# A part of the attention exponentials by integer writes on VectorE, shifted copies on GpSimd and a sum on TensorE, in a conformer block

## The chip, the core and the metric

The kernel runs on one core of a Trainium2 chip, in one launch. A core has five engines, each with its own queue of instructions, which it takes in order: TensorE (PE in the profile; its weight loads stand apart as PEld), VectorE (DVE), ScalarE (ACT), GpSimd (POOL) and SyncE (SP, which here only issues DMAs). Matrix products land in PSUM, 128 partitions by 8 banks of 512 fp32 numbers; everything else lives in SBUF. The metric is device time in microseconds, the median of the runs.

## What is computed

Two sequences of 4000 tokens with 144 channels pass a conformer block. Cut to its steps:

```python
B, T, D, K, H = (2, 4000, 144, 5, 4)          # head size 36
h = _layernorm(x);  x = x + 0.5 * (_silu(h @ w_ff1a) @ w_ff1b)      # inner size 576
h = _layernorm(x);  q, k, v = split_heads(h @ w_qkv)
scores = jnp.einsum('bhqd,bhkd->bhqk', q, k) * scale
p = _softmax(scores)
att = jnp.einsum('bhqk,bhkd->bhqd', p, v)
x = x + att @ w_o
h = _layernorm(x) @ w_pw1;  a, b = halves(h)
h = a * _sigmoid(b)
c = depthwise convolution of h with 5 taps, dw
x = x + _silu(c) @ w_pw2
h = _layernorm(x);  x = x + 0.5 * (_silu(h @ w_ff2a) @ w_ff2b)
return _layernorm(x)
```

The scores are 2 x 4 x 4000 x 4000 numbers, and each needs an exponential. No maximum is subtracted ahead of it in the kernel.

## The kernel before

**Tiles.** The 8000 tokens are 16 chunks of 500 (`CH`), eight to a sequence; a chunk is four blocks of 125 tokens (`TB`, `NB`). Attention runs in 32 groups: sequence, query chunk, pair of heads (`groups`). A group walks over 32 key tiles of 125 keys (`NKT`). For one key tile PE makes the scores of 125 keys by 500 queries for two heads with four matmuls (`emit_S`: each head's 64 padded channels take half of the rows of the array, 64 and 61 keys take half of its columns each, so the four lie on different quarters). They go to two PSUM banks; two such pairs, banks 0 to 3, take turns. ACT writes their exponential as bf16 into `PT`, 125 x 1000 in one instruction (`emit_exp`). Four more matmuls multiply by the values `VA` (36 channels and a column of ones, padded to 64) and add up in banks 4 and 5 over the whole group (`emit_O`).

**Epilogue.** At the end of a group, `epilogue` adds banks 4 and 5 on DVE in two instructions (`OTA`, `OTF`), transposes in fp32 on PE, divides by the sum that the column of ones gave, and after the second head pair hands the chunk to `post1` (output projection, norm, gated unit into `U`). `post2` does convolution, second projection, norm, feed-forward, last norm and store. Chunks of the second sequence pass `ff1` and `pre2` (norm, projections to `QT`, `KT`, `VA`) while the first one's attention runs.

**The norm.** `ln` takes statistics on DVE (`ST`, `MV`), raises the variance to the power -1/2 on POOL (two instructions on `RS`), and scales two blocks on DVE into `XN`. There are 160 such half chunks.

**Silu.** While exponentials run, silu and sigmoid are made from tanh (`TH` on ACT, then one DVE instruction), since tanh and exp share a table. Before the attention and after it (`mode["front"]`, `mode["tail"]`) ACT makes silu itself.

**Order.** Nothing is scheduled at run time. A planner, written in Python (`Rec`, `Sched`), writes out the order of each engine before the program is built: every step is a generator that asks for an engine and perhaps a slot; each instruction carries a guessed `cost`, each engine a latency (`LAT`); the step that could start first by these guesses is emitted next. Waits between engines follow from the data. An instruction that comes later than guessed therefore holds up what stands behind it on its engine. During attention only banks 6 and 7 (`banks.restrict`) are left for all side work. All instructions are recorded through one helper, so the profile puts nearly all of them on one line (L135), and they are told apart by the names of their tiles.

**The main loop** alternates between the next score tile and side work. The scores of tile n wait for the exponential of tile n-2. Two series, one of even and one of odd chunks, run `post2`; each takes one chunk to its end before the next. What is left of them when the last key tile is out is emitted after the loop, with all eight banks free. `U` holds all eight chunks of a sequence, `QT` all queries.

Of the kernel before, what the change touches and what calls it, by code (L numbers as in the profile page):

```python
# [6 lines left out]
ALU = mybir.AluOpType  # L7
BF16 = mybir.dt.bfloat16
F32 = mybir.dt.float32

# [10 lines left out]
ATT_SCALE = 0.1669921875  # L21

# [5 lines left out]
class Rec:  # L28
# [5 lines left out]
    LAT = dict(pe=0.2, act=0.2, dve=0.12, pool=0.08, sp=2.0)  # L34
# [10 lines left out]
    def op(self, eng, name, *a, r=(), w=(), q=None, cost=0.1, kind=None, **k):  # L45
# [21 lines left out]
        if eng == "pe":  # L67
            if kind != self.kind:
                start += 0.13
            self.kind = kind  # L70
# [177 lines left out]
def bass_standalone__conformer_family_zipformer__speech_kernel(  # L248
# [29 lines left out]
    NPT = 6  # L278
# [10 lines left out]
    QT = sb("QT", [2, N])  # L289
    KT = sb("KT", [2, N])  # L290
    VA = sb("VA", [NBLK, H, 64])
    PT = sb("PT", [NPT, 2, CH])
    OTA = sb("OTA", [CH], F32)
# [3 lines left out]
    U = sb("U", [CPB, 2, NB, 128])  # L297
# [75 lines left out]
    def va_init(c):  # L373
        blks = slice(c * NB, (c + 1) * NB)
        op("dve", "memset", VA[:, blks, :, DH + 1:64], 0.0, w=[("VA0", c)], cost=0.2)
        op("dve", "memset", VA[:, blks, :, DH:DH + 1], 1.0, w=[("VA1", c)], cost=0.1)
# [54 lines left out]
    def ln(c, g):  # L431
        u = yield need("dve", xnp)
        for i in range(2):
            op("dve", "bn_stats", ST[0:TB, u, i, :], X[0:TB, c * NB + 2 * g + i, :], r=[("X", c, 2 * g + i)],
               w=[("ST", u, i)], cost=0.233)
        yield need("dve")
        for i in range(2):
            op("dve", "bn_aggr", MV[0:TB, u, i, :], ST[0:TB, u, i, :], r=[("ST", u, i)], w=[("MV", u)], cost=0.09)
        op("pool", "tensor_scalar", RS[0:TB, u, :, 1], MV[0:TB, u, :, 1], LN_EPS, None, op0=ALU.add,
           r=[("MV", u)], w=[("VE", u)], cost=0.25)  # L440
        op("pool", "tensor_tensor", RS[0:TB, u, :, 0], RS[0:TB, u, :, 1], NHALF[0:TB, :], op=ALU.pow,
           r=[("VE", u), "NHALF"], w=[("RS", u)], cost=0.6)
        yield need("dve")
        for i in range(2):
            op("dve", "tensor_scalar", XN[0:TB, u, i, :], X[0:TB, c * NB + 2 * g + i, :], MV[0:TB, u, i, 0:1],
               RS[0:TB, u, i, 0:1], op0=ALU.subtract, op1=ALU.mult, r=[("X", c, 2 * g + i), ("MV", u), ("RS", u)],
               w=[("XN", u)], cost=0.25)
        return u
# [64 lines left out]
    def proj(Tt, Wt, nm, c, s, p):  # L513
# [6 lines left out]
        copy(Tt[:, p, c * CH:(c + 1) * CH], PSV[:, bk, 0:CH], [("ps", bk)], [(nm + "T", c)], 0.62, 0.47)  # L520
        banks.give(bk)

    def vproj(c, s, g):
        bk = yield need("pe", banks)
        for i in (2 * g, 2 * g + 1):
            for k in range(2):
# [6 lines left out]
             [("ps", bk), ("VA0", c), ("VA1", c)], [("VA", c)], 0.42, 0.3)  # L533
# [4 lines left out]
    att_done = set()  # L538
# [15 lines left out]
    def pre2(c):  # L554
        s = yield need("dve", xtp, cond=lambda: c in ff1_done)
# [7 lines left out]
        kv_done.add(c)  # L563

    def glu(c, s, hf):
        cc = c % CPB
# [7 lines left out]
        op("dve", "scalar_tensor_tensor", out=U[0:HD, cc, hf, :, 1:1 + TB],  # L574
           in0=TH[0:HD, t, :].rearrange("p (i n) -> p i n", i=NB), scalar=1.0,
           in1=PSV[0:HD, bk, 0:CH].rearrange("p (i n) -> p i n", i=NB), op0=ALU.add, op1=ALU.mult,
           r=[("TH", t), ("ps", bk)], w=[("U", cc)], cost=0.63)
# [3 lines left out]
    def post1(c, a):  # L581
# [13 lines left out]
        yield need("pe", kids=kids, cond=lambda: b == 0 or min(c - CPB + 1, CPB - 1) in conv_done)  # L595
# [4 lines left out]
        xtp.give(s2)  # L600
        if cc == 0:
            op("pool", "memset", U[0:HD, cc, :, 2:4, 0:1], 0.0, w=[("UL", cc)], cost=0.1)
        else:
            op("pool", "tensor_copy", U[0:HD, cc, :, 2:4, 0:1], U[0:HD, cc - 1, :, 2:4, TB:TB + 1],
               r=[("U", cc - 1)], w=[("UL", cc)], cost=0.25)
            op("pool", "tensor_copy", U[0:HD, cc - 1, :, 0:2, TB + 1:TB + 2], U[0:HD, cc, :, 0:2, 1:2],
               r=[("U", cc)], w=[("UR", cc - 1)], cost=0.25)
        if cc == CPB - 1:
            op("pool", "memset", U[0:HD, cc, :, 0:2, TB + 1:TB + 2], 0.0, w=[("UR", cc)], cost=0.1)
        glu_done.add(c)  # L610

    def conv(c, z, hf, silu):
        cc = c % CPB
        bk = yield need("pe", banks)
        o = PSV[0:HD, bk, 0:CH].rearrange("p (i n) -> p i n", i=NB)
        u = U[0:HD, cc, hf, :, :]
        parts = [(2, 0, 4, 0, 1), (1, 1, 4, 0, 1), (1, 0, 1, 3, 0), (0, 2, 4, 0, 1), (0, 0, 2, 2, 0),
                 (3, 0, 3, 1, 1), (3, 3, 4, 0, 2), (4, 0, 2, 2, 1), (4, 2, 4, 0, 2)]
        for j, (tap, i0, i1, s0, off) in enumerate(parts):
            op("pe", "matmul", o[:, i0:i1, :], lhsT=DG[0:HD, hf, tap, :], rhs=u[:, s0:s0 + i1 - i0, off:off + TB],  # L620
               start=j == 0, stop=j == len(parts) - 1, r=[("U", cc), ("UL", cc), ("UR", cc), "DG"], w=[("ps", bk)],
# [49 lines left out]
    def epilogue(b, qc, p, gi):  # L671
        c = b * CPB + qc
        op("dve", "tensor_copy", OTA[:, :], PSV[:, 4, 0:CH], r=[("ps", 4)], w=["OTA"], cost=0.62)
        op("dve", "tensor_tensor", OTF[:, gi % 2, :], PSV[:, 5, 0:CH], OTA[:, :], op=ALU.add, r=[("ps", 5), "OTA"],
           w=[("OTF", gi % 2)], cost=0.62)
# [4 lines left out]
        if p == 0:  # L680
            an_of[c] = yield need("dve", anp)
        a = an_of[c]
        yield need("dve")
# [13 lines left out]
    its = [(gi, kt) for gi in range(len(groups)) for kt in range(NKT)]  # L697
    halves = ((0, 64), (64, TB))
    exps = {}

    def emit_S(n):
        gi, kt = its[n]
        b, qc, p = groups[gi]
        k0 = b * T + kt * TB
        q0 = b * T + qc * CH
        kc, qcc = b * CPB + kt // NB, b * CPB + qc
        for m0, m1 in halves:
            for hh in range(2):
                op("pe", "matmul", PSV[m0:m1, 2 * (n % 2) + hh, 0:CH],
                   lhsT=KT[64 * hh:64 * hh + 64, p, k0 + m0:k0 + m1], rhs=QT[64 * hh:64 * hh + 64, p, q0:q0 + CH],  # L710
                   start=True, stop=True, skip_group_check=True, r=[("WKT", kc), ("WQT", qcc)],
                   w=[("ps", 2 * (n % 2) + hh)], cost=0.0525, kind="q")

    def emit_exp(n):
        s = 2 * (n % 2)
        exps[n] = op("act", "activation", PT[0:TB, n % NPT, :, :], PSV[0:TB, s:s + 2, 0:CH], ACT.Exp, bias=0.0,
                     scale=ATT_SCALE, r=[("ps", s), ("ps", s + 1)], w=[("PT", n % NPT)], cost=0.883)

    def emit_O(n):
        gi, kt = its[n]  # L720
        b, qc, p = groups[gi]
        blk = b * NKT + kt
        for r, (m0, m1) in enumerate(halves):
            for hh in range(2):
                op("pe", "matmul", PSV[64 * hh:64 * hh + 64, 4 + r, 0:CH], lhsT=VA[m0:m1, blk, 2 * p + hh, :],
                   rhs=PT[m0:m1, n % NPT, hh, :], start=kt == 0, stop=kt == NKT - 1, skip_group_check=True,
                   r=[("PT", n % NPT), ("VA", blk // NB)], w=[("ps", 4 + r)], cost=0.0525, kind="q")
        if kt == NKT - 1:
            S.add(epilogue(*groups[gi], gi), first=True)

    def s_start(n):

        gi, kt = its[n]
        b, qc, p = groups[gi]
        kc = b * CPB + kt // NB
        if kc not in kv_done:
            return None
        t = max(R.free["pe"], R.ready(("WKT", kc)), R.ready(("WQT", b * CPB + qc)))
        return max(t, exps[n - 2].done) if n >= 2 else t
# [12 lines left out]
    NIT = len(its)  # L752
    pend = []
    n_s = 0
    n_e = 0
    later = [False]

    def emit_pending(force=False):
        while pend:
            m = pend[0]  # L760
            first = its[m][1] == 0
            t = max(exps[m].done, max(R.ready(("OTF", 0)), R.ready(("OTF", 1))) if first else 0.0)
# [4 lines left out]
    while n_e < NIT:  # L767
        a = s_start(n_s) if n_s < NIT else R.free["pe"]
        t, th = S.best()
        if th is not None and (a is None or t < a or (th.req[0] == "act" and t < a + 0.05)):  # L770
# [8 lines left out]
        assert a is not None, "nothing can go on"  # L779
        if n_s < NIT:  # L780
            emit_S(n_s)
            n_s += 1
        if n_s >= 2 or n_s == NIT:
# [3 lines left out]
            n_e += 1  # L787
    mode["tail"] = True
    emit_pending(force=True)
# [39 lines left out]
```

## Time and profile before

| | |
|---|---|
| median of 3 runs | 1153.02 us |
| the runs | 1148.37 to 1153.84 us |
| span of the profiled execution, first to last instruction | 1145.6 us |
| start of the first exponential | 58.2 us |
| end of the last exponential | 1096.8 us |
| mean granted clock of TensorE | 0.977 |
| HBM read and written | 3.26 MB and 2.30 MB |

The profile gives the profiled execution's span; no other time of that execution is known, and the runs were timed without it. A row of instructions gives engine, operation, written tile and tiles read, shapes, count, then busy time and the mean length of one in ns, then the idle time just before them and who ended it. Instructions of one engine may overlap: the length of one is longer than the distance between the starts of two, for ACT by its pipeline and for PE because a matmul's last rows are still under way when the next one starts. So a price per instruction is read from starts, not from lengths.

### The profile page before, as it was taken

The page shows a single profiled execution, that of the slowest core. Times are in us where ns is not written, and L with a number is a line of the kernel's source. Part 1 is how long each engine was busy: PE and PEld are TensorE (multiplying, and loading weights), DVE is VectorE, ACT ScalarE, POOL GpSimd, SP SyncE. Part 2 cuts the span into 40 slices and gives each one's busy share as a digit, 9 for nine tenths or more (in the row PEclk, how much of TensorE's full clock was granted, in tenths as well). Part 3 has the DMA queues.
Part 4 walks back from the last instruction along what each step waited for, and adds up shares of the span by engine and source line. Part 5 has one row for each costly group of instructions (what it writes and reads, how often), then busy time and mean ns, then how long its engine had stood idle before and what let it go on. Part 6 is the DMA issues. An engine that isn't in the chain of part 4 may idle for free.

```text
span 1145.6 us, 25298 instructions
## 1 busy us (share of the span) xinstructions
PE 959.3 (84%) x10886; PEld 367.5 (32%) x10886; DVE 526.4 (46%) x1657; ACT 1060.9 (93%) x1290; POOL 153.9 (13%) x359
## 2 busy tenths in 40 slices
PE   8998888999999987887879887878878787978766
PEld 3632333333433332322323321322223232323224
DVE  5975655666766643342424520433424241424324
ACT  3789999999999999999999999999999999999942
POOL 3420101111211110010001100100100010101002
PEclk8999999999999999999999999999999999999966
DMA  3000000000000000000000000000000000000000
GB/s 115 2 1 1 1 2 1 1 2 1 7 1 1 7 6 6 2 6 2 1 6 1 9 5 1 1 6 1 6 2 1 6 2 6 2 6 1 6 1 11
DMA packets 8514, 7.18 MB, mean 6 GB/s; under 512 B 1826, under 2 KB 8402, under 8 KB 8402
## 3 DMA queue, kind: packets, MB, share of 16 engines
q1 hardware_dynamic: 7482, 5.11, 1.5%
q8 instruction: 85, 1.39, 0.5%
q10 hardware_dynamic: 920, 0.46, 0.2%
q14 instruction: 27, 0.22, 0.1%
HBM read 3.26 MB, written 2.30 MB: 5 GB/s over the span
## 4 chain that ended last, share of the span: by engine, by line
ACT 68%; PE 23%; DVE 5%; POOL 2%; issue 1%; DMA 1%; ACTq 0%; POOLq 0%; DVEq 0%
ACT PT L135 61%; PE PS L135 23%; ACT TH L135 6%; DVE HT L135 1%; POOL RS L135 1%; DVE XN L135 1%; DVE U L135 1%; DMA WQKV<-in_w_qkv_dram 1%; DVE ST L135 0%; DVE X L135 0%; ACT QT L135 0%; DVE MV L135 0%; DVE VA L135 0%; DVE OTF L135 0%; ACT XT L135 0%
## 5 line engine op out<-in xcount | busy, mean ns | idle before, releaser
L135 ACT ACTIVATE PT<-PS 125x1000 bf16<-125x1000 f32 x1024 | 953.5, 1071 | 12.6 <-PE PS L135 10.3
L135 PE MATMUL PS<-QT,KT 64*64 64x500 bf16 (+1 forms) x4096 | 413.0, 393 | 130.5 <-ACT PT L135 126.5
L135 PE MATMUL PS<-PT,VA 61*64 61x500 bf16 (+1 forms) x4096 | 387.7, 372 | 0.8 <-ACT PT L135 0.8
L135 PEld LDWEIGHTS PS<-QT,KT 64*64 64x64 bf16 (+1 forms) x4096 | 115.4, 103 | 464.4 <-ACT PT L135 424.2
L135 POOL TENSOR_SCALAR RS<-MV 125x2 f32<-125x2 f32 x160 | 34.9, 218 | 883.6 <-DVE MV L135 883.0
L135 PEld LDWEIGHTS PS<-PT,VA 61*64 61x64 bf16 (+1 forms) x4096 | 119.1, 106 | 10.8 <-DVE OTF L135 3.1
L135 DVE COPY OTA<-PS 128x500 f32<-128x500 f32 x32 | 21.7, 679 | 218.0 <-PE PS L135 217.9
L135 POOL TENSOR_TENSOR RS<-RS,NHALF 125x2 f32<-125x2 f32 x160 | 113.9, 712 | 13.4
L135 ACT ACTIVATE TH<-PS 128x500 bf16<-128x500 f32 (+1 forms) x170 | 107.1, 630 | 6.3 <-PE PS L135 6.2
L135 DVE SCALAR_TENSOR_TENSOR HT<-TH,PS 128x500 bf16<-128x500 bf16 x110 | 72.9, 672 | 78.9 <-ACT TH L135 78.8
L135 DVE TENSOR_SCALAR XN<-X,MV,RS 125x144 bf16<-125x144 bf16 x320 | 86.6, 313 | 48.3 <-POOL RS L135 47.5
L135 PE MATMUL PS<-XT,WA 72*128 72x500 bf16 x320 | 93.7, 398 | 9.3 <-DVE HT L135 7.0
L135 DVE SCALAR_TENSOR_TENSOR X<-PS,X 125x288 bf16<-125x288 f32 x128 | 57.2, 448 | 57.0 <-PE PS L135 56.7
L135 DVE BATCH_NORM_STATS2 ST<-X 125x6 f32<-125x144 bf16 x320 | 81.4, 296 | 2.8
L135 DVE COPY XT<-PS 72x500 bf16<-72x500 bf16 x143 | 57.7, 413 | 43.6 <-PE PS L135 43.1
L135 PE MATMUL PS<-WB,HT 128*125 128x144 bf16 x640 | 52.7, 234 | 9.7 <-DVE HT L135 8.8
L135 PE MATMUL PS<-IDENT,XN 125*72 125x125 bf16 x512 | 50.9, 228 | 11.7 <-DVE XN L135 9.3
L135 PEld LDWEIGHTS PS<-WB,HT 128*125 128x125 bf16 x640 | 45.5, 141 | 29.4 <-DVE HT L135 17.3
L135 PEld LDWEIGHTS PS<-IDENT,XN 125*72 125x72 bf16 x512 | 33.7, 115 | 55.9 <-DVE XN L135 32.2
L135 DVE SCALAR_TENSOR_TENSOR U<-TH,PS 72x500 bf16<-72x500 bf16 x32 | 21.5, 671 | 60.0 <-ACT PT L135 30.5
L135 PE MATMUL PS<-U,DG 72*72 72x250 bf16 (+3 forms) x288 | 44.1, 305 | 4.5 <-POOL U L135 3.8
L135 PEld LDWEIGHTS PS<-XT,WA 72*128 72x128 bf16 x320 | 23.4, 101 | 69.0 <-DVE HT L135 29.7
(55 smaller groups left out, 495.0 us busy)
## 6 DMA issues: line engine op xcount, KB each, us to landing
X<-in_x_dram SPq DMA_DIRECT2D x16, 140.6 KB
out_dram<-XN SPq DMA_DIRECT2D x32, 70.3 KB
WA<-in_w_ff1a_dram ACTq DMA_DIRECT2D x1, 162.0 KB
WA<-in_w_ff2a_dram SPq DMA_DIRECT2D x1, 162.0 KB
WB<-in_w_ff1b_dram ACTq DMA_DIRECT2D x1, 144.0 KB
WB<-in_w_ff2b_dram SPq DMA_DIRECT2D x1, 144.0 KB
WQKV<-in_w_qkv_dram ACTq DMA_DIRECT2D x1, 121.5 KB
WP<-in_w_pw_dram SPq DMA_DIRECT2D x1, 81.0 KB
```

The source lines that it names most:

```text
L135: ins = getattr(eng, o.name)(*o.a, **o.k)
```

## The change

134 of the 1024 key tiles leave ACT. They are taken from the last eight key tiles of a group (`NDV`), and are called far tiles here, after the new function `far_tiles`. For such a tile:

- PE makes the scores in banks 6 and 7, which the side work also uses; if only one is free, one head first and the other later.
- DVE computes `LERP_A * score + LERP_B` and writes it as a 16-bit unsigned integer into `PD`, one instruction of 125 x 500 per head. Read as bf16, whose exponent starts at bit 7, such an integer is 2 to a power that is linear in the score, with the fraction replaced by a straight line.
- POOL writes three copies with 32, 64 and 96 added, that is, shifted by a quarter, a half and three quarters of an octave.
- PE multiplies the four with the values and with three scaled copies of the values (`VD`, weights `LERP_W`), sixteen matmuls in all, so that the mean of four shifted lines stands for the exponential. `VD` is made on POOL once for each sequence, for its last eight key tiles.

The planner decides which tile goes this way and when, with two such tiles in flight (`NPD`) and not before the first sequence's keys are all there. Together with this:

- In `ln` the scaling into `XN` moves from DVE to POOL.
- The epilogue's two DVE instructions become one `tensor_reduce` over both banks.
- `VA` keeps 38 columns in place of 64, the output matmuls write 37, and the zero columns aren't set any more; banks 4 and 5 are cleared once by two dummy matmuls.
- `U` holds four chunks (`NUS`) and `QT` twelve (`NQS`), both as rings, and `post1` and `pre2` wait for a free place.
- The order of the four score matmuls is by head, then by half. Some guessed costs and latencies of the planner are new, and the tiles' order in a group may differ.

```diff
-    LAT = dict(pe=0.2, act=0.2, dve=0.12, pool=0.08, sp=2.0)
+    LAT = dict(pe=0.2, act=0.2, dve=0.12, pool=0.15, sp=2.0)
...
+LERP_W = (0.83984375, 0.70703125, 0.59375)
+LERP_A = ATT_SCALE * 128.0 / 0.6931471805599453
+LERP_B = 125.0 * 128.0 - 7.2342
...
-    NPT = 6
+    NPT, NPD, NUS, NQS = 6, 2, 4, 12
+    JT = 4
+    NDV = 8
+    MINREM = 8
+    LEAD = -2
...
-        yield need("dve")
         for i in range(2):
-            op("dve", "tensor_scalar", XN[0:TB, u, i, :], ...
+            op("pool", "tensor_scalar", XN[0:TB, u, i, :], ...
...
     def pre2(c):
...
+        b, k0 = c // CPB, (c % CPB) * NB - (NKT - NDV)
+        if k0 >= 0:
+            for j in range(1, JT):
+                yield need("pool")
+                op("pool", "tensor_scalar", VD[0:TB, b, j - 1, k0:k0 + NB, :, 0:DH + 1],
+                   VA[0:TB, c * NB:(c + 1) * NB, :, 0:DH + 1], LERP_W[j - 1], None, op0=ALU.mult,
+                   r=[("VA", c), ("VA1", c)], w=[("VD", b)], cost=0.8)
+            vd_done.add(c)
...
     def epilogue(b, qc, p, gi):
-        op("dve", "tensor_copy", OTA[:, :], PSV[:, 4, 0:CH], ...
-        op("dve", "tensor_tensor", OTF[:, gi % 2, :], PSV[:, 5, 0:CH], OTA[:, :], op=ALU.add, ...
+        op("dve", "tensor_reduce", out=OTF[:, gi % 2, :], in_=PSV[:, 4:6, 0:CH].rearrange("p b n -> p n b"),
+           axis=mybir.AxisListType.X, op=ALU.add, ...
...
+    def far_tiles(u):
+        while next_tile() is not None or mode["front"]:
+            bk = yield need("pe", banks, cond=lambda: far_tile() is not None)
+            gi, kt = far_tile(take=True)
+            b, qc, p = groups[gi]
+            both = banks.free and banks.best() <= R.free["pe"] + 0.15
+            bks = [bk, banks.take()] if both else [bk]
+            for hh in range(len(bks)):
+                scores(gi, kt, bks[hh], hh)
+            for hh in range(2):
+                if hh == len(bks):
+                    bks.append((yield need("pe", banks)))
+                    scores(gi, kt, bks[hh], hh)
+                yield need("dve")
+                op("dve", "tensor_scalar", PD[0:TB, u, 0, hh, :], PSV[0:TB, bks[hh], 0:CH], LERP_A, LERP_B,
+                   op0=ALU.mult, op1=ALU.add, r=[("ps", bks[hh])], w=[("PD", u)], cost=0.64)
+                banks.give(bks[hh])
+            for j in range(1, JT):
+                yield need("pool")
+                op("pool", "tensor_scalar", PD[0:TB, u, j, :, :], PD[0:TB, u, 0, :, :], float(32 * j), None,
+                   op0=ALU.add, r=[("PD", u)], w=[("PD", u, j)], cost=0.95)
+            vk = kt - (NKT - NDV)
+            pd = PD[:, u, :, :, :].bitcast(BF16)
+            yield need("pe", cond=lambda: o_grp[0] == gi and o_left[gi] < NKT)
+            outputs(gi, [(VA[...] if j == 0 else VD[...], pd[:, j, :, :]) for j in range(JT)], ...)
+            output_done(gi)
```

More of the change, by code (lines that the diff above doesn't have):

```diff
@@ L719, in emit_O @@
     def emit_O(n):
-        gi, kt = its[n]
+        gi, kt = tiles[n]
         b, qc, p = groups[gi]
         blk = b * NKT + kt
[L723 to L727, printed above, removed]
@@ L778, in bass_standalone__conformer_family_zipformer__speech_kernel @@
             continue
[L779 to L783, printed above, removed]
+        assert a is not None and not full, "nothing can go on"
+        more = next_tile() is not None
+        if more:
+            emit_S()
+        if len(tiles) >= 2 or not more:
             emit_exp(n_e)
```

187 lines of the change are left out of this document (127 added, 60 removed).

## The prediction

> **What bounds the kernel now.** I read the page's busy times and groups first, then the windows by stage, then the timeline of a quiet and of a crowded stretch, and the chain of waits at the end.
>
> ```profile
> span 1145.6 us, 25298 instructions
> ...
> PE 959.3 (84%) x10886; PEld 367.5 (32%) x10886; DVE 526.4 (46%) x1657; ACT 1060.9 (93%) x1290; POOL 153.9 (13%) x359
> ...
> L135 ACT ACTIVATE PT<-PS 125x1000 bf16<-125x1000 f32 x1024 | 953.5, 1071 | 12.6 <-PE PS L135 10.3
> ...
> L135 POOL TENSOR_SCALAR RS<-MV 125x2 f32<-125x2 f32 x160 | 34.9, 218 | 883.6 <-DVE MV L135 883.0
> ...
> L135 POOL TENSOR_TENSOR RS<-RS,NHALF 125x2 f32<-125x2 f32 x160 | 113.9, 712 | 13.4
> ...
> L135 DVE TENSOR_SCALAR XN<-X,MV,RS 125x144 bf16<-125x144 bf16 x320 | 86.6, 313 | 48.3 <-POOL RS L135 47.5
> ```
>
> ACT is the full engine, and 1024 exponentials fill it. POOL is nearly empty. The windows (columns: PE, PEld, DVE, ACT, POOL busy, then the granted clock) cut the span at the start of the first exponential, at the end of the first group of 32 key tiles, and at the end of the last exponential; two single groups follow.
>
> ```profile
> 58.20:102.00 43.80, 38.81 (x398) 14.99 (x398) 30.59 (x111) 37.71 (x51) 9.41 (x20) 1.00 0.00 1
> 102.00:1096.80 994.80, 837.28 (x9928) 301.30 (x9925) 432.95 (x1276) 977.37 (x1161) 111.98 (x261) 1.00 0.01 3
> 1096.80:1145.60 48.80, 30.80 (x168) 19.61 (x168) 20.85 (x79) 13.14 (x22) 9.66 (x23) 0.59 0.02 6
> 333.20:367.90 34.70, 32.75 (x367) 12.70 (x364) 21.63 (x59) 34.01 (x44) 4.05 (x10) 1.00 0.01 2
> 685.20:714.30 29.10, 20.29 (x260) 5.32 (x260) 2.02 (x4) 28.81 (x34) 0.00 (x0) 1.00 0.01 1
> ```
>
> So there are three parts: 102.0 us up to the end of the first group, 994.8 us of loop (31 groups), 48.8 us of tail. In the loop ACT is busy 977 of 995. The quiet stretch gives the prices:
>
> ```profile
> 699.78 9.14 ACT L135 ACTIVATE PT<-PS 125x1000 bf16<-125x1000 f32 x10
> ...
> 700.01 0.41 PE L135 MATMUL PS<-QT,KT 64*64 64x500 bf16 x4 [0.28 <-ACT PT L135]
> ...
> 700.25 0.38 PE L135 MATMUL PS<-PT,VA 64*64 64x500 bf16 x4
> ```
>
> Ten exponentials of 1.071 us each take 9.14 us, so they start every (9.14 - 1.07)/9 = 0.897 us. PE waits for ACT. The tanh instructions of the loop, and what one adds to ACT in the chain of waits:
>
> ```profile
> 102.00:1096.80 994.80, 105.91 (x168) 1.00 0.01 3
> ```
>
> ```profile
> 1066.16 0.48 ACT TH L135
> ```
>
> ACT's floor in the loop is 992 x 0.897 + 168 x 0.475 = 890 + 80 = 970 us. The loop's 995 is 2.6% above it.
>
> **The change, part by part.** The order of instructions in the changed program, counted without times, has 890 exponentials in place of 1024 (32 in the first group, 858 in the loop) and 149 tanh in the loop instead of 168. *ACT's floor* becomes 858 x 0.897 + 149 x 0.475 = 770 + 71 = 841 us: 129 us less. The question is what takes part of that back.
>
> *TensorE.* Start-to-start times of a crowded stretch:
>
> ```profile
> 364.32 0.38 PE L135 MATMUL PS<-PT,VA 64*64 64x500 bf16 x4
> ...
> 364.53 0.38 PE L135 MATMUL PS<-QT,KT 64*64 64x500 bf16 x4
> ...
> 365.06 1.47 PE L135 MATMUL PS<-WB,HT 128*125 128x144 bf16 x20
> ...
> 366.45 0.40 PE L135 MATMUL PS<-QT,KT 64*64 64x500 bf16 x4
> ...
> 367.43 1.26 PE L135 MATMUL PS<-U,DG 72*72 72x500 bf16 x9
> ...
> 368.62 0.40 PE L135 MATMUL PS<-QT,KT 64*64 64x500 bf16 x4
> ...
> 370.91 0.41 PE L135 MATMUL PS<-IDENT,XN 125*72 125x125 bf16 x4
> 371.25 0.41 PE L135 MATMUL PS<-QT,KT 64*64 64x500 bf16 x4
> ```
>
> ```profile
> 320.60 0.60 PE L135 MATMUL PS<-XT,WA 72*128 72x500 bf16 x2 [0.24 <-DVE HT L135]
> 321.12 0.41 PE L135 MATMUL PS<-QT,KT 64*64 64x500 bf16 x4
> ```
>
> Four output matmuls hold PE 0.21 us, four score matmuls 0.24, so a tile costs 0.45 of ACT's 0.897. Ten WB matmuls cost 0.70, a convolution of nine 1.19, four small transposes 0.34, a 500-column pair 0.52. A far tile (one that leaves ACT) has four score matmuls and sixteen output matmuls: 0.24 + 4 x 0.21 = 1.08 us. In the new order 69 of the 134 have their two heads apart, with other work between, so that only two matmuls run side by side: 69 x 0.21 = 14 us more. Together 134 x 1.08 + 14 = 159 us. The other tiles take 858 x 0.45 = 386. The side work of the loop counts 115 + 70 sets of four small matmuls (63), 187 pairs (97), 38 WB tens (27), 24 convolutions (29) and 31 fp32 transposes of four, which I put at twice the small ones (21): 237 us. PE's sum is 782 us; the same count for before is 446 of tiles and 259 of side work, 705.
>
> How far above ACT's floor does a loop come that is so full on PE? The windows answer: group 333.2 to 367.9 has ten tanh, floor 32 x 0.897 + 10 x 0.475 = 33.5, and took 34.7, 3.6% more, with PE by the same prices about 85% full (14.4 us of its 32 tiles and 15 us of side work). The quiet group (29.1 against 28.7) is 1.4% over. After the change the mean loop is at 782/880 = 89%, beyond the most crowded group of before. I take 4.5% over the floor: 841 x 1.045 = 879 us. Bounds: 2.6% as now (863), and 12% (942), where every far tile adds (942 - 863)/134 = 0.6 us of idle ACT because PE stands in order behind its wait.
>
> *VectorE.* It gains 268 evictions of 125x500 from PSUM and loses all 320 scalings XN (86.6 us). Nearest rows:
>
> ```profile
> L135 DVE CAST KT<-PS 128x500 bf16<-128x500 f32 x27 | 18.3, 678 | 13.8 <-PE PS L135 13.7
> ...
> L135 POOL COPY U<-U 72x4 bf16<-72x4 bf16 x28 | 5.6, 199 | 90.8 <-DVE U L135 90.8
> ...
> L135 POOL TENSOR_SCALAR_AFFINE_SELECT IDENT<-IDENT 128x128 bf16<-128x128 bf16 x1 | 0.3, 294 | 0.2 <-POOL IDENT L135 0.2
> ```
>
> 268 x 0.68 = 182 us, so DVE is busy near 433 + 182 - 70 = 545 of 879 us in the loop. Not a bound. The 0.68 us hold banks 6 and 7, which the side work shares; that wait is inside the 4.5%. The two-step sum of an epilogue becomes one reduction of 1000 elements; by the cast's 0.68 us per 500 it lies between 0.68 and 1.36 against 1.36 now, so it is at worst even. The cleared columns of VA go; they lay beside PE-bound work in the front.
>
> *GpSimd.* The trace shows no 1000-element instruction there. From 4 to 128 elements (199 to 294 ns) the slope is 0.77 ns per element: 0.97 us for a shifted copy. Lower bound, slope from the 218 ns of the two-element row: 0.82. Upper, the select's 294 ns per 128 with no fixed part: 2.30. I take 0.97, since the select also reads and writes 16-bit data and its fixed part is seen in the small rows. XN of 144 elements is then 0.33 (0.33 to 0.55). The loop holds 107 half-chunk norms: 107 x (0.22 + 0.71 + 2 x 0.33 + 0.16 of gaps) = 187 us, 402 copies = 390, the twelve scaled V blocks and the small copies 14: 591 of 879 us, 67%. The output matmuls of a far tile stand 4 to 16 exponentials behind its scores in the order, 9 in the middle, some 8.5 us; the path (0.4 scores, 2 x 0.68, 3 x 0.97, some 0.2 of hand-over) is 4.9. So the median tile isn't waited for, those at 4 and 5 are.
>
> By the Trainium skill, "GPSIMD Engine Reference", § 3.1, a tight loop on these cores takes about 1.8 cycles an element at best, while § 4.1 calls one-input work about line-rate; the first would make a copy 1.5 us (an estimate from that page) and GpSimd's sum 804 of 879 us, the second fits the 0.77 ns slope. The row decides for me; the first is the direction of the second rival.
>
> *Before the loop.* 33 norms send their scaling to GpSimd; each is two instructions of 0.33 on the slower queue in place of 0.31 on DVE, and PE fills that stage (38.8 of 43.8 us). Only the first one or two are exposed: 102 + 1 = 103 us.
>
> *The tail.* Here the order says most: after the last output matmul it now has feed-forward work of five chunks (25 silu), not two (10), and four chunks' convolutions, not two. Chain of waits before:
>
> ```profile
> 1075.17 21.63 ACT PT L135 x24
> ...
> 1113.29 9.54 PE PS L135 x44
> ...
> 1123.48 0.75 PE PS L135 x4
> ...
> 1133.57 0.47 DVE X L135
> ```
>
> From the last exponential to the convolutions 16.5 us, then 20.7 for two chunks side by side up to the last residual (1134.0), then 11.6 for the last norm and store. In the new order chunk 11's feed-forward hides in the first piece; chunks 12 and 13 go side by side (20.7); the convolution of 14 stands on PE behind 13's last WB matmul, and that of 15 behind 14's. A chunk alone is half of 9.54 plus 0.6 for its activation plus 1123.48 to 1134.0: 15.9 us, two of them 31.8. Sum 16.5 + 20.7 + 31.8 + 11.6 = 80.6 us. Bounds: 62 if 14 and 15 still run side by side, 90 if the twenty norms at 1.75 us queue on GpSimd. I take 80.
>
> The granted clock in this window is 0.59, against 1.00 in the loop. By the Trainium skill, "TensorE: Matmul & The Clock Gate", Part 1, PE runs at half clock after an idle window of about 3.4 us; a fuller tail could stay at full clock, which by halving the 9.5 us pieces would make it nearer 70.
>
> **Sum.** 103 + 879 + 80 = 1062 us against a span of 1145.6. The median of the runs, 1153.0, lies 7.4 above the span; with the same, 1069.
>
> **Rivals.** (1) *PE's waits decide.* The far tiles' sixteen matmuls wait for the third copy, and everything behind them on PE, the next scores first, waits too; ACT starves. For it: PE at 89%, two far tiles share two banks and one GpSimd queue. Against it: two score buffers, and the distances above. At 0.6 us a tile: 103 + 942 + 80 + 7 = 1132.
>
> (2) *GpSimd becomes the bound: slower than before.* Its sum in the loop is 402c + 201 us for a copy of c. The change breaks even where that is 1145.6 - 103 - 80 = 963, at c = 1.9 us. At 2.0 it gives 1005 + 183 + 7 = 1195. For it: no row above 128 elements, integers may go another way than bf16. Against: the slope.
>
> (3) *ACT stays the only bound and the tail overlaps.* 102 + 863 + 62 + 7 = 1034. For it: a planner lays out order and tail. Against: PE's load.
>
> (4) *It doesn't do what it says:* the exponentials leave ACT, but each far tile idles it as long as one lasted. The tail's 31 us are then lost outright; from 0.64 us a tile beyond today's share it is a loss. This is rival 1 driven further, near 1150.
>
> **Chances.** Forecast 0.57 (own range 1045 to 1095), rival 1 0.16, rival 2 0.09, rival 3 0.13, rival 4 0.05. The range takes in rivals 1 and 3: 1030 to 1135, leaving out rivals 2 and 4 and a little of 3. Faster or slower means beyond 0.5%, about what a measurement of this kernel tells from none. Rival 4 lies around no change: 0.01 of it faster, 0.03 same, 0.01 slower. Faster: 0.57 + 0.16 + 0.13 + 0.01 = 0.87; same 0.03; slower 0.09 + 0.01 = 0.10.
>
> **What would show it.** Right: exponentials still 0.89 to 0.90 us apart, 890 of them; ACT over 92% busy in a loop near 880 us; the shifted copies at 0.8 to 1.1 us and GpSimd at 60 to 70%; last exponential near 980; a tail near 80 us with 25 silu. Wrong: ACT waiting for PE's scores for more than 60 us in all (rival 1); GpSimd over 90% or copies over 1.5 us (rival 2); a tail under 65 us (rival 3); evictions far from 0.68 us.

## The result, and the profile after

The changed kernel takes 1813.01 us, median of 4 runs (1803.41 to 1831.58), against 1152.61 us for the kernel before beside it: a ratio of 1.569, 95% interval 1.557 to 1.580. It is 57% slower; the forecast was 1069 us, 7% faster. The ratio is one of fast runs: it leaves out the slowest of the four, 1831.58 us, which is the one that was profiled (span 1829.8 us).

From the page of the changed kernel: busy times, the chain of waits by engine, and the groups that answer to those shown of before.

```profile
span 1829.8 us, 29034 instructions
...
PE 1254.2 (69%) x12496; PEld 501.1 (27%) x12496; DVE 597.5 (33%) x1542; ACT 978.4 (53%) x1152; POOL 1525.5 (83%) x1093
...
POOL 76%; PE 18%; DVE 3%; issue 2%; ACT 1%; DMA 0%; ACTq 0%; POOLq 0%; DVEq 0%
...
L140 ACT ACTIVATE PT<-PS 125x1000 bf16<-125x1000 f32 x890 | 854.0, 1009 | 665.1 <-PE PS L140 662.4
L140 POOL TENSOR_SCALAR PD<-PD 125x1000 uint16<-125x1000 uint16 x402 | 1079.6, 2712 | 80.9 <-DVE PD L140 77.1
...
L140 PE MATMUL PS<-PD,VA 64*37 64x500 bf16 (+1 forms) x536 | 70.7, 513 | 426.9 <-POOL PD L140 426.9
L140 DVE TENSOR_SCALAR PD<-PS 125x500 uint16<-125x500 f32 x268 | 173.2, 674 | 468.0 <-PE PS L140 466.3
L140 POOL TENSOR_SCALAR XN<-X,MV,RS 125x144 bf16<-125x144 bf16 x320 | 271.5, 856 | 16.9
...
L140 DVE TENSOR_REDUCE OTF<-PS 128x500 f32<-128x1000 f32 x32 | 38.4, 1200 | 116.4 <-PE PS L140 116.3
```

A shifted copy takes 2.71 us, not 0.97, and a scaling into XN 0.86 us, not 0.33. GpSimd's busy time alone, 1525 us, is longer than the whole kernel before. Nobody else is full: ACT, once 93% busy, stands still for 662 us behind scores that PE hasn't made, and PE for 427 us behind copies that GpSimd hasn't made, as its list of waits counts them (total, times, longest):

```profile
PE PS L140 <- POOL PD L140: 426.9, 113, 10.8
```

The windows of the changed kernel, cut as before at the first exponential, the end of the first group and the end of the last exponential (columns: PE, PEld, DVE, ACT, POOL busy, granted clock):

```profile
0.00:72.20 72.20, 54.12 (x387) 32.97 (x388) 33.50 (x164) 29.60 (x54) 58.18 (x95) 0.86 0.15 46
```

```profile
72.20:139.70 67.50, 65.65 (x412) 21.61 (x410) 27.20 (x72) 37.88 (x47) 36.62 (x49) 0.57 0.00 1
139.70:1722.80 1583.10, 1072.57 (x11374) 406.79 (x11372) 508.63 (x1194) 884.44 (x1008) 1374.07 (x863) 0.79 0.01 2
1722.80:1829.80 107.00, 61.85 (x326) 39.72 (x326) 28.19 (x112) 26.53 (x46) 56.59 (x89) 0.57 0.03 9
```

The three parts that were forecast as 103, 879 and 80 us are 139.7, 1583.1 and 107.0. Of the 684 us over the span of before (1829.8 - 1145.6), 588 came in the loop, 38 ahead of it and 58 in the tail.

One stall, from the timeline of the changed kernel (start, length, engine, work, and in brackets the idle time before and who ended it):

```profile
1318.76 1.39 DVE L140 TENSOR_SCALAR PD<-PS 125x500 uint16<-125x500 f32 x2
...
1319.53 16.12 POOL L140 TENSOR_SCALAR PD<-PD 125x1000 uint16<-125x1000 uint16 x6 [1.03 <-DVE PD L140]
...
1321.90 0.40 PE L140 MATMUL PS<-QT,KT 64*64 64x500 bf16 x4
...
1322.13 0.38 PE L140 MATMUL PS<-PT,VA 64*37 64x500 bf16 x4
...
1330.35 0.61 PE L140 MATMUL PS<-PD,VA 64*37 64x500 bf16 x4 [6.12 <-POOL PD L140]
...
1332.00 0.63 PE L140 MATMUL PS<-QT,KT 64*64 64x500 bf16 x4
...
1332.42 0.63 PE L140 MATMUL PS<-PT,VA 64*37 64x500 bf16 x4
...
1332.68 1.00 ACT L140 ACTIVATE PT<-PS 125x1000 bf16<-125x1000 f32 x1 [6.71 <-PE PS L140]
...
1333.50 0.68 DVE L140 TENSOR_SCALAR PD<-PS 125x500 uint16<-125x500 f32 x1 [7.71 <-PE PS L140]
...
1335.71 0.61 PE L140 MATMUL PS<-PD,VA 64*37 64x500 bf16 x4 [2.25 <-POOL PD L140]
...
1338.03 2.79 ACT L140 ACTIVATE PT<-PS 125x1000 bf16<-125x1000 f32 x3 [4.34 <-PE PS L140]
```

Six copies run without a gap, 16.12 / 6 = 2.69 us each. In the program's order the copies of the two tiles in flight are mixed here: the fourth of the six is the third of one tile, the sixth the third of the other. PE comes to a far tile's output matmuls and waits 6.1 us, until the fourth has ended at 1319.53 + 4 x 2.69 = 1330.3; the next far tile waits for the sixth. The scores behind these matmuls wait too, so ACT stands for 6.7 us and DVE, which could evict the next far tile, for 7.7. Behind the wait PE is also slower: four matmuls take 1332.42 - 1332.00 = 0.42 us from start to start, against 1322.13 - 1321.90 = 0.23 ahead of it, and the sixteen matmuls of the far tile 1332.00 - 1330.35 = 1.65 us where 0.84 was forecast. By the Trainium skill, "TensorE: Matmul & The Clock Gate", Part 1, PE falls to half clock after about 3.4 us of idling; the trace agrees, here and in the granted 0.79 of the loop (1.00 before).

### The profile page after: what moved, and what is told of

It is laid out like the page before. It is cut to its first block, busy times and chain, and to the rows that moved or that the text cites. A ratio compares the mean times of both kernels' runs of the same rounds, so it can differ in the third digit from the quotient of the medians.

```text
span 1829.8 us, 29034 instructions
## 1 busy us (share of the span) xinstructions
PE 1254.2 (69%) x12496; PEld 501.1 (27%) x12496; DVE 597.5 (33%) x1542; ACT 978.4 (53%) x1152; POOL 1525.5 (83%) x1093
## 4 chain that ended last, share of the span: by engine, by line
POOL 76%; PE 18%; DVE 3%; issue 2%; ACT 1%; DMA 0%; ACTq 0%; POOLq 0%; DVEq 0%
POOL PD L140 57%; PE PS L140 18%; POOL XN L140 12%; POOL RS L140 7%; DVE PD L140 1%; DVE ST L140 1%; POOL VD L140 1%; DVE X L140 1%; DMA WQKV<-in_w_qkv_dram 0%; DVE MV L140 0%; ACT PT L140 0%; ACT HT L140 0%; DVE OTF L140 0%; DVE QT L140 0%; DVE U L140 0%
## 5 line engine op out<-in xcount | busy, mean ns | idle before, releaser
L140 ACT ACTIVATE PT<-PS 125x1000 bf16<-125x1000 f32 x890 | 854.0, 1009 | 665.1 <-PE PS L140 662.4
L140 POOL TENSOR_SCALAR PD<-PD 125x1000 uint16<-125x1000 uint16 x402 | 1079.6, 2712 | 80.9 <-DVE PD L140 77.1
L140 PE MATMUL PS<-QT,KT 64*64 64x500 bf16 (+1 forms) x4096 | 491.4, 465 | 21.0 <-ACT PT L140 16.8
L140 PE MATMUL PS<-PT,VA 64*37 64x500 bf16 x3560 | 411.8, 446 | 1.0 <-ACT PT L140 0.5
L140 PE MATMUL PS<-PD,VA 64*37 64x500 bf16 (+1 forms) x536 | 70.7, 513 | 426.9 <-POOL PD L140 426.9
L140 DVE TENSOR_SCALAR PD<-PS 125x500 uint16<-125x500 f32 x268 | 173.2, 674 | 468.0 <-PE PS L140 466.3
L140 POOL TENSOR_SCALAR XN<-X,MV,RS 125x144 bf16<-125x144 bf16 x320 | 271.5, 856 | 16.9
L140 PE MATMUL PS<-PD,VD 64*37 64x500 bf16 (+1 forms) x1608 | 163.4, 526 | 0.0
L140 PEld LDWEIGHTS PS<-PT,VA 64*37 64x37 bf16 x3560 | 113.6, 112 | 67.3 <-issue 43.9
L140 DVE TENSOR_REDUCE OTF<-PS 128x500 f32<-128x1000 f32 x32 | 38.4, 1200 | 116.4 <-PE PS L140 116.3
```

What stands on the lines that cost most here:

```text
L140: ins = getattr(eng, o.name)(*o.a, **o.k)
```

## The experiments

All ratios are to the kernel before, run beside.

**What a GpSimd instruction costs.** The kernel before, with GpSimd instructions by themselves behind its end, two of each kind; its time says nothing.

> The kernel before, with GpSimd instructions alone on scratch tiles after its end, two of each shape, and at last two of them beside VectorE copies. Theory (the price is GpSimd's own, about 2.5 ns per element and 0.2 fixed for this kind of instruction): integer add of 1000 elements 2.7 us, 500 elements 1.45, 128 elements 0.5, also for bf16; the select and the memset stay near 0.8 ns per element, which is why they misled. Rival (the length comes from VectorE working beside it): alone near 1.0 us, and longer only beside the VectorE copies. Time near 1190 us, which says nothing.

Groups of that run, from windows cut so that a kind stands in one of them:

```profile
L135 POOL TENSOR_SCALAR QT<-QT 125x1000 uint16<-125x1000 uint16 x2 | 5.4, 2719 | 9.1 <-DVE QT L135 9.0
...
L135 POOL TENSOR_SCALAR QT<-QT 125x128 uint16<-125x128 uint16 x2 | 1.1, 528 | 0.2
L135 POOL TENSOR_SCALAR QT<-QT 125x32 uint16<-125x32 uint16 x2 | 0.6, 288 | 0.2
...
L135 POOL TENSOR_SCALAR QT<-QT 125x1000 bf16<-125x1000 bf16 x2 | 5.4, 2714 | 0.2
...
L135 POOL COPY QT<-QT 125x1000 bf16<-125x1000 bf16 x2 | 2.0, 1016 | 0.1
L135 POOL MEMSET QT<- 125x1000 bf16 x2 | 1.9, 931 | 0.1
...
L135 POOL TENSOR_SCALAR_AFFINE_SELECT QT<-QT 125x500 bf16<-125x500 bf16 x2 | 1.2, 602 | 0.3
...
L135 POOL TENSOR_TENSOR QT<-QT 125x500 int32<-125x500 int32 x1 | 1.2, 1234 | 0.1
```

The copy's price is the instruction's own: 2.72 us alone at the end as in the loop. From 32 and 1000 elements, (2719 - 288)/968 = 2.51 ns an element and 0.21 us fixed. The type doesn't matter (bf16 the same). A plain copy, a memset and the select cost 0.9 to 1.2 ns an element with all that is fixed in them, near the forecast's slope of 0.77: the select row priced a select about rightly and an addition wrongly. And 500 additions of 32-bit integers, which carry the same 1000 16-bit numbers, cost 1.23 us. The norm's scaling has a price of its own too: on 144 elements the run's last rows give 0.57 us with one constant and 0.85 us with the two operands per partition that `XN` needs.

**Cheap copies, nothing else changed.** Same order, memsets in place of the copies.

```diff
-op("pool", "tensor_scalar", PD[0:TB, u, j, :, :], PD[0:TB, u, 0, :, :], float(32 * j), None, ...
+op("pool", "memset", PD[0:TB, u, j, :, :].bitcast(BF16), 0.0, ...
```

> The changed kernel, its order kept instruction by instruction, with each of the 402 shifted copies replaced by a GpSimd memset of the same 125x1000 tile, so that the far tiles' outputs lack three of four terms. Theory (the length of the copies is what the time goes into): memset near 0.9 us, GpSimd no longer full, time 1070 to 1130 us. Rival (the order of PE, banks and far tiles costs the time whatever the copies take): above 1500 us.

```profile
L140 POOL MEMSET PD<- 125x1000 bf16 x402 | 357.2, 933 | 109.2 <-DVE PD L140 108.6
```

A memset takes 933 ns, nearly the price forecast for a copy. Time 1161.38 us, ratio 1.004 (1.000 to 1.009): some 650 us of the loss go with the copies' price alone. But neither the forecast nor the 1070 to 1130 named for this run is reached: with copies at the forecast price the change is worth nothing while XN is on GpSimd.

**No far tiles, with and without XN on GpSimd.**

```diff
     def far_tile(take=False):
         nt = next_tile()
-        if mode["front"] or nt is None:
-            return None
+        return None
```

> The changed kernel without far tiles: all 1024 exponentials on ACT; the norm scaling on GpSimd, the reduction in the epilogue, the narrow V and the rings stay. Theory (only far tiles cost): 1145 to 1175 us, GpSimd near 440 us busy. Rival (the scaling at 0.85 us on GpSimd also costs, by late norms that hold up PE): above 1200 us.

> The changed kernel without far tiles and with the norm scaling back on VectorE: the reduction in the epilogue, the narrow V, the rings and the new guesses of the planner are all that is left of the change. Theory (the 110 us of the kernel without far tiles come from the scaling at 0.85 us on GpSimd): 1145 to 1160 us, as before. Rival (rings, reduction or order cost something of their own): above 1180 us.

In the second run XN is back on DVE, so that what is left are the small edits:

```diff
-op("pool", "tensor_scalar", XN[0:TB, u, i, :], ...
+op("dve", "tensor_scalar", XN[0:TB, u, i, :], ...
```

1264.82 us (ratio 1.094, 1.074 to 1.115) and 1161.88 (1.007, 1.002 to 1.011). So the move of XN costs about 103 us by itself, and reduction, narrower values and rings together at most 1.1%. Where most of it goes is in PE's waits of the first run; the wait for ACT is that of before (127.2 us), the one for XN is new:

```profile
PE PS L140 <- ACT PT L140: 125.0, 393, 1.0
PE PS L140 <- POOL XN L140: 82.8, 76, 3.8
```

A norm's two scalings last 1.7 us on GpSimd, and the transposes that read them stand in PE's queue ahead of scores.

**XN back on DVE, far tiles and copies as changed.**

> The changed kernel with only the norm scaling back on VectorE; 131 far tiles with their 393 copies stay on GpSimd. Theory (GpSimd's sum sets the time): GpSimd falls by 270 us to 1240 busy, time 1400 to 1550 us. Rival (the time is set by late order, not by the sum): little changed, above 1700 us.

1706.06 us (1.476, 1.457 to 1.495): 107 less than the change, some 100 again. GpSimd's sum alone doesn't set the time; it stands idle for 478 us of the 1707.8:

```profile
PE 1202.1 (70%) x12460; PEld 490.8 (29%) x12460; DVE 682.1 (40%) x1853; ACT 979.1 (57%) x1163; POOL 1229.6 (72%) x764
```

**The planner told the true prices.**

```diff
-w=[("PD", u, j)], cost=0.95)
+w=[("PD", u, j)], cost=2.7)
-w=[("XN", u)], cost=0.4)
+w=[("XN", u)], cost=0.84)
-w=[("VD", b)], cost=0.8)
+w=[("VD", b)], cost=1.7)
```

> The changed kernel, in which the planner is told GpSimd's measured prices (2.7 us a copy, 0.84 a scaling, 1.7 a scaled V block) and so plans 93 far tiles in place of 134; work and engines stay the same. Theory (GpSimd's throughput): 279 x 2.72 + 444 = 1203 us of GpSimd are still needed, time 1250 to 1400 us. Rival (only the order, written for copies of 0.95 us, loses the time): near 1100 us.

1634.62 us (1.414, 1.395 to 1.434), far above what either theory named for the run. The planner takes 93 far tiles in place of 134 and still loses: wrong guesses in the order alone don't make the loss, and GpSimd's 1194 us of work in that run don't either.

**The copies on DVE.** The planner is told 0.4 us a copy, and 0.35 in the second run, in which XN is on DVE too.

```diff
-yield need("pool")
-op("pool", "tensor_scalar", PD[0:TB, u, j, :, :], ..., cost=0.95)
+yield need("dve")
+op("dve", "tensor_scalar", PD[0:TB, u, j, :, :], ..., cost=0.4)
```

> The changed kernel with the shifted copies on VectorE in place of GpSimd, planned at 0.4 us each. Theory: a copy of 1000 16-bit elements in SBUF takes VectorE 0.35 to 0.45 us, GpSimd falls to 450 us, ACT is the full engine again: 1070 to 1120 us. Rival (the far tiles are too dear on PE and on banks 6 and 7 as well): above 1153 us with ACT waiting for PE.

> Copies and XN both on VectorE, planned at 0.35 us a copy: 117 far tiles (351 copies) and 907 exps. VectorE's copy takes 0.42 us: 147 us more on it, near 800 busy in all, and none of it waits for GpSimd's long instructions. If only GpSimd's prices broke the forecast, this holds its mechanism as well as the integer additions on GpSimd did: ScalarE's floor 907 x 0.897 + 79 = 893, PE about 90% busy: 1095 to 1130. If VectorE, now with LayerNorm, evictions and copies in one queue, delays the banks, it is 1140 to 1180, as with copies alone on VectorE (1185, of which XN on GpSimd takes some 35).

```profile
L140 DVE TENSOR_SCALAR PD<-PD 125x1000 uint16<-125x1000 uint16 x384 | 142.0, 419 | 3.9
```

A copy takes 419 ns there. With XN left on GpSimd the time is 1184.84 us (1.025, 1.011 to 1.039), in the rival's range, but XN's price is in it; with XN on DVE as well it is 1141.52 (0.987, 0.979 to 0.995). The second lies where delayed banks were to put it, but its windows of loop and tail tell another cause:

```profile
101.80:998.00 896.20, 812.98 (x10890) 332.23 (x10888) 603.78 (x1578) 859.45 (x996) 102.67 (x212) 0.99 0.01 3
998.00:1139.60 141.60, 105.33 (x604) 68.79 (x604) 71.72 (x277) 47.50 (x83) 35.56 (x81) 0.63 0.03 9
```

The loop ends at 998.0, 99 us earlier than before (1096.8); the tail, 48.8 before, is 141.6, since the planner left more side work behind the last key tile (604 matmuls there against 168). Of the 99 us gained 93 are given back there.

**The copies as 32-bit integer additions on GpSimd, XN on DVE.** Each copy adds a constant tile, 32 in both halves of every word, to the copy before it; the integers are those of the change. Told 1.25 us a copy, the planner takes 123 far tiles.

```diff
-op("pool", "tensor_scalar", PD[0:TB, u, j, :, :], PD[0:TB, u, 0, :, :], float(32 * j), None, ...
+op("pool", "tensor_tensor", PD[0:TB, u, j, :, :].bitcast(I32), PD[0:TB, u, j - 1, :, :].bitcast(I32),
+   SH[0:TB, :].rearrange("p (o n) -> p o n", o=1).to_broadcast([TB, 2, CH // 2]), op=ALU.add, ..., cost=1.25)
```

> Norm scaling back on VectorE, and the shifted copies made on GpSimd as 500 32-bit integer additions of a constant tile, 1.25 us each by the price row, planned so; 123 far tiles. The result is the same to the bit. Theory: GpSimd at 620 us no longer bounds, ACT does, with PE close: 1060 to 1110 us, faster than before. Rival (far tiles don't pay even when GpSimd keeps up, since PE and the two banks can't take them): 1150 us or more.

1102.95 us, ratio 0.954 (0.943 to 0.966): faster than the kernel before by 4.6%, and the fastest of all. From its page and its windows:

```profile
PE 995.4 (90%) x12364; PEld 435.3 (40%) x12364; DVE 697.5 (63%) x1839; ACT 969.2 (88%) x1171; POOL 597.8 (54%) x741
...
PE 55%; ACT 31%; DVE 10%; issue 1%; POOL 1%; DMA 1%; ACTq 0%; POOLq 0%; DVEq 0%
...
L141 ACT ACTIVATE PT<-PS 125x1000 bf16<-125x1000 f32 x901 | 851.5, 1028 | 41.6 <-PE PS L141 36.6
L141 POOL TENSOR_TENSOR PD<-PD,SH 125x500 int32<-125x500 int32 x369 | 425.1, 1158 | 189.7 <-DVE PD L141 174.3
```

```profile
58.60:101.80 43.20, 39.75 (x402) 14.26 (x402) 29.83 (x96) 37.55 (x49) 17.88 (x24) 1.00 0.00 1
101.80:1030.60 928.80, 854.02 (x11294) 357.66 (x11294) 594.55 (x1425) 876.20 (x1026) 540.54 (x625) 0.99 0.01 4
1030.60:1099.90 69.30, 49.28 (x270) 31.52 (x270) 31.88 (x126) 22.49 (x38) 16.41 (x37) 0.60 0.03 9
```

With copies of 1.16 us, still 20% dearer than forecast, GpSimd is 54% busy, ACT waits 37 us for PE's scores in place of 662, and the clock is back at 0.99. Against this run the change's 729.9 us more of span are 471 more of PE idle (575.6 against 104.5) and 259 more of PE busy (1254.2 against 995.4, for about the same matmuls at a clock of 0.771 against 0.963 over the span).

**Half the far tiles.** XN on DVE, at most two far tiles a group.

```diff
-            if g < len(groups) and len(left[g]) > MINREM:
+            if g < len(groups) and len(left[g]) > MINREM and taken[g] < 2:
```

> Every group gives at most two of its key tiles to the far path (64 at most, where the run with XN on VectorE had 131); the rest as in that run, XN on VectorE. GpSimd's sum is 192 copies x 2.71 + some 180 = 700 us of a loop of about 1030, so GpSimd has slack on average. Theory 'a far tile stalls PE': the planner puts a far tile's output matmuls at the time of a 0.95 us copy, three copies take 8.1, and PE waits the difference at each tile whatever GpSimd's mean load is. Then each tile costs what it cost there, (1706 - 1162) / 131 = 4.15 us, and the time is 1162 + 64 x 4.15 = 1428 (1350 to 1470). Theory 'GpSimd's sum alone': with 700 us GpSimd is no bound any more, ScalarE's 960 exps are, and the time is 1090 to 1150. In between (1150 to 1350) both take part.

62 far tiles, 186 copies, 1336.74 us (1.156, 1.143 to 1.168): between the theories. PE waited only 9.6 us in all for copies, which speaks against the first, and GpSimd is 50% busy with a time far over 1150, against the second. Other waits stand out in the lists of DVE and PE:

```profile
DVE XN L140 <- POOL RS L140: 134.0, 48, 13.7
```

```profile
PE PS L140 <- POOL U L140: 51.8, 11, 5.5
PE PS L140 <- POOL PD L140: 9.6, 2, 5.2
```

LayerNorm's factor RS is made on GpSimd and stands there behind copies, up to 13.7 us; DVE, in order, waits for it with evictions behind it. PE waits in the same way for the convolution's edge copies (`U`).

**The copies not read.** All far tiles, XN on DVE.

```diff
-VD[:, b, j - 1, vk, 2 * p:2 * p + 2, :], pd[:, j, :, :]) for j in range(JT)],
+VD[:, b, j - 1, vk, 2 * p:2 * p + 2, :], pd[:, 0, :, :]) for j in range(JT)],
...
-+ [("PD", u, j) for j in range(1, JT)])
+)
```

> The run with XN on VectorE (1706 us) once more, all far tiles and all copies on GpSimd, but the output matmuls of a far tile read the original four times and none of the shifted copies (the output is not the reference's). PE no longer waits for a copy; GpSimd still makes all 393, and a buffer still comes free only after its copies. Theory 'PE in order': PE standing at a far tile's output matmuls is why the time is longer than GpSimd's sum, so the time falls to that sum: 1153 us of work from 100 to 1600 in that run, 1160 to 1200 for the loop, with 100 before and 80 after it 1340 to 1400 in all, GpSimd over 95% busy in the loop. Rival 'the copies alone': PE's wait is an echo of GpSimd, which is starved by VectorE and by banks for its share; the time stays at 1640 to 1720. Third way, below 1250: GpSimd's sum isn't a bound either, only PE's waiting is.

1557.31 us (1.346, 1.332 to 1.361): 149 less than with the copies read, not the 300 that "PE in order" claimed, nor the nothing of its rival.

**GpSimd's queue left to the copies.** To take the new waits away, RS and the convolution's edge copies go to DVE as well: with half the far tiles, with all, and with all and the copies not read. These kernels leave the power out: the norm's factor is a constant 1.

```diff
-op("pool", "tensor_scalar", RS[0:TB, u, :, 1], MV[0:TB, u, :, 1], LN_EPS, None, op0=ALU.add, ...
-op("pool", "tensor_tensor", RS[0:TB, u, :, 0], RS[0:TB, u, :, 1], NHALF[0:TB, :], op=ALU.pow, ...
+op("dve", "tensor_scalar", RS[0:TB, u, :, 0], MV[0:TB, u, :, 1], 0.0, 1.0, op0=ALU.mult, op1=ALU.add, ...
...
-op("pool", "tensor_copy", U[0:HD, us, :, 2:4, 0:1], ...
+op("dve", "tensor_copy", U[0:HD, us, :, 2:4, 0:1], ...
```

> The run with half the far tiles (1337 us, 62 of them) with GpSimd's queue left to the copies and VD: XN, LayerNorm's factor and the convolution's edge copies on VectorE. VectorE has no power, so the factor is a constant 1 of one instruction in place of the addition and the power (the output is not the reference's). Theory 'queue': in the run before VectorE waited 134 us for RS (48 times, longest 13.7) and PE 52 us for U behind copies; without these the 186 copies (504 us) are hidden, and the time is 1120 to 1180. Rival 'PE in order': PE's place and the copies' length are unchanged, so the time stays at 1300 to 1340; PE's wait for PD was 9.6 us only, which speaks against it.

> The run with all far tiles and XN on VectorE (1706 us), with GpSimd's queue left to the copies and VD in the same way (LayerNorm's factor is a constant 1, the output is not the reference's). GpSimd's sum is 393 x 2.71 + 20 = 1085 us, which begins at about 105 and has a tail of 75 behind it: no less than 1265. Theory 'queue': the excess was the queue, the time is 1270 to 1400 and GpSimd over 90% busy in the loop. Theory 'PE in order': PE still stands at each far tile's matmuls (356 us, 98 times) and GpSimd still waits for the next far tile's evictions meanwhile: 1520 to 1640, less than before by the 160 us of the removed GpSimd work at most. In between both take part.

> Both taken away: GpSimd's queue holds only the copies and VD, and PE reads the original four times and no copy (neither the factor nor the far tiles' sums are the reference's). GpSimd's sum, 1085 us, is then all that is left of the change's slow part: with 105 before and 75 after it 1265 to 1330, GpSimd over 93% busy in the loop. If it stays above 1400, VectorE's wait for a buffer (evictions of the far tile after next, behind six copies, 193 us with the copies unread) is a third wait that holds its queue, and with two buffers the copies can't be hidden even then.

1148.37 us (0.992, 0.986 to 0.997), 1667.16 (1.442, 1.421 to 1.463) and 1491.66 (1.290, 1.271 to 1.309). With the runs before, all with XN on DVE (no far tiles: 1162):

| us | GpSimd's queue shared | copies alone on it |
|---|---|---|
| half the far tiles (62), copies read | 1337 | 1148 |
| all (128 to 131), copies read | 1706 | 1667 |
| all (130 to 132), copies not read | 1557 | 1492 |

With half the tiles the shared queue is the whole loss, 188 us, about the 134 + 52 us of the two waits above; 186 copies of 2.7 us are then hidden. (That the power is gone as well is not separated from it. It can't be much: without far tiles and with XN on DVE, where the power is still made, DVE waited 26.6 us for RS in all.) With all, the queue is worth 39 us, and 1667 lies above both ranges named for that run; PE's reading is worth 149, both together 214. What stays in the last run, 330 us over no far tiles, is neither. A part of it is GpSimd's own work: with the time ahead of it and behind it, its sum was put at 1265 to 1330 of the 1492 us, and it was busy for 1081. The rest is in DVE's and PE's waits of that run:

```profile
DVE PD L140 <- POOL PD L140: 324.4, 76, 8.1
```

```profile
PE PS L140 <- DVE PD L140: 240.3, 89, 6.6
```

DVE waits 324 us to evict into a buffer whose copies aren't made yet, and PE 240 for the banks behind that eviction. This was the third way named for that run. Take PE's wait away, and the same lateness comes out at DVE. The far tile's copies take 8.1 us, two buffers are all there are, and whoever holds the next place in an order written ahead stands still for them. This last step is read from the waits; no run had a third buffer.

## Why the prediction was wrong

*GpSimd's copy: the step that failed.* 0.97 us came from a slope between a select of 128 and a copy of four elements; the copies are additions with a scalar, at 2.71 us. The bounds, 0.82 to 2.30, were also taken from unlike instructions and didn't hold it. The only additions with a scalar in the trace of before had two elements, and showed the fixed part alone. Nothing there excluded 2.5 ns an element, and the 0.09 given to the second rival was too little for a price that no row showed. By the Trainium skill, "GPSIMD Engine Reference", § 4.1, one-input work is about line-rate: the plain copy's 1016 ns agrees, the addition's 2719 doesn't, and the measurement decides; the 1.5 us estimated from § 3.1 was too low as well.

*XN on GpSimd.* 0.33 (at most 0.55) was forecast, 0.856 measured, and it is a price of its own: about 103 us without a single far tile. The memset run shows that copies as cheap as forecast don't save the gain with it (1161 us). No run has memsets and XN on DVE; the nearest, integer copies of 1.16 us with XN on DVE, takes 1103.

*The second rival, GpSimd as bound, happened, and was under-priced.* With the measured prices its own sum for the loop is 402 x 2.71 + 107 x (0.23 + 0.72 + 2 x 0.86 + 0.16) + 14 = 1089 + 303 + 14 = 1406 us, and 1374 were busy. The loop took 1583: the 209 us of idle GpSimd were not in that rival. They are the waits in order of the table: GpSimd starves while PE, which waits for GpSimd, can't make the next scores.

*"The median far tile isn't waited for"* fell with the price: the path of 4.9 us becomes 0.4 + 1.4 + 8.1 + 0.2 = 10.1, against the 8.5 us the order left. PE waited 113 times for 134 far tiles, 426.9 us. That is the first rival's mechanism, so both came, one out of the other.

*Ahead of the loop* +1 us was forecast, with PE as cover. The first exponential is 14.0 us later (72.2 against 58.2): GpSimd is busy 58.2 of those 72.2 us, and norms, not PE, lead there. With XN on DVE the first exponential is back at 58.6. The first group is another 23.7 us longer, and that is not GpSimd but PE's clock: PE is busy 65.65 of the 67.5 us at a granted 0.57, and from 72.2 to 130 us it is granted 0.50 while it stands still for 0.1 us in all. The memset run has the same instructions up to here, with the same scalings on GpSimd; its first exponential is at 72.0, its clock from there on 1.00, and its first group takes 45.3 us. So some 22 us of the loss shown are the clock's, and why it stayed low is open. (In the run without far tiles and with XN on GpSimd it was 0.50 from 72 to 100 us too.)

*The tail* was to be 80, at most 90, with 25 silu. It had those 25 and took 107; PE waited 28 us there for XN. The bound had the norms at 1.75 us; with 0.86 us a scaling they take 2.8. With XN on DVE and 20 silu it was 69.

*Two sums.* The slope puts a scaling of 144 elements at 0.31 us, not 0.33. The fourth rival's limit of 0.64 us a tile comes out as (963 - 863) / 134 = 0.75 from its own terms. Neither changes the outcome.

*What held:* 890 exponentials, (2.79 - 1.00) / 2 = 0.895 us apart when PE is in time; evictions of 0.674 us; a reduction of 1.20 us, no dearer than the two steps before; and, once the copies and XN are repaired, a gain of the kind forecast. Even then the loop was mis-sized: the integer run's 869 exponentials and 156 tanh of the loop make a floor of 869 x 0.897 + 156 x 0.475 = 854 us, and the loop took 928.8, 8.8% more, where 4.5% was taken and 12% allowed. Both PE (854 us) and ACT (876) are over 90% busy in that loop; PE leads the chain of waits with 55% to ACT's 31%.

## What to carry to other kernels

Price an instruction from a row of the same operation at some size; a row of another operation, even on the same engine and type, bounded nothing here, and where no row exists the chance of an ugly price has to be large. Before an engine that looks empty is given long instructions, list who waits for the short ones already in its queue. Where the order is written ahead and an intermediate has two buffers, a producer that is late stops its reader, and if the reader is spared, the writer of the next one.

## What the runs showed of the hardware

GpSimd's price goes by operation, not by bytes: 2.72 us for adding a scalar to 1000 16-bit numbers, 1.02 for copying them, and 1.16 to 1.23 for adding 500 32-bit words of the same size, with two inputs.

GpSimd and DVE held each other up in one place. In the timeline of the pricing run DVE's additions stand alone at first, then beside plain copies on GpSimd; the copies alone come first:

```profile
1185.45 2.09 POOL L135 COPY QT<-QT 125x1000 bf16<-125x1000 bf16 x2
...
1200.14 1.78 DVE L135 TENSOR_SCALAR QT<-QT 125x1000 uint16<-125x1000 uint16 x4 [31.00 <-POOL QT L135]
...
1202.09 4.99 DVE L135 TENSOR_SCALAR QT<-QT 125x1000 uint16<-125x1000 uint16 x8
1202.12 2.41 POOL L135 COPY QT<-QT 125x1000 bf16<-125x1000 bf16 x2 [2.01 <-DVE QT L135]
```

Eight additions would take 2 x 1.78 = 3.56 us and took 4.99; the two copies took 2.41 in place of 2.09. The change's evictions, whose source is PSUM, show nothing of it: they last 674 ns beside GpSimd's copies and 673 with the copies on DVE. With XN on DVE its scalings, from SBUF to SBUF, do: 365 ns beside the 393 copies against 311 without far tiles.

The wait has a second price that no sum of durations holds: in the change PE's busy time is 259 us longer than in the integer run, for about the same matmuls at a lower granted clock. In the loop no run separates the clock from the waits that come with it. The first group does: with the same instructions it took 67.5 us at a granted 0.57 in the change, PE busy for 65.65, and 45.3 at 1.00 in the memset run, PE busy for 40.4. A clock that has fallen can thus stay down for 58 us of unbroken work.
